# Attention units of batches 1 to 3: third tile first, 1/sum one unit later, two PSUM banks borrowed from the transposes

## The chip, the cores and the metric

The kernel runs on one core of a Trainium2 chip. The metric is the device time of one execution in microseconds (us), from launch to end on that core. TensorE is called PE below, its weight loads PEld, VectorE DVE, ScalarE ACT, GpSimd POOL, and SyncE (which only issues DMAs here) SP.

## The reference

The program computes an attention and two dense layers on top of it; shapes are q, k, v = (4 batches, 8 heads, 1152, 64).

```python
q_pool = q.reshape(B, H, S // 2, 2, D).mean(axis=3)        # 576 pooled queries
scores = scale * np.matmul(q_pool, k.transpose(0, 1, 3, 2))
attn = np.exp(scores - max) ; attn = attn / (attn.sum(-1) + 1e-9)
x = np.matmul(attn, v)                                     # heads side by side: (2304, 512)
h = x @ w_in ; g = where(h >= 1, h, where(h <= -1, 0, (h + 1) ** 2 / 4)) ; y = g @ w_out
out = np.maximum(np.maximum(y @ w1, y @ w2), y @ w3) @ w_out2
```

## The kernel before

**Units.** The attention is cut into 48 units: batch b (4), block i of 192 pooled queries (3), pair of heads p (4). A unit has three score tiles of 128 rows by 1152 keys. Tiles 0 and 1 hold 128 queries of one head each; tile 2 holds the remaining 64 queries of both heads. Numbers are kept as pairs of fp16 (a high part and a rest), so products are made of three matmuls.

**Words of a unit.** The order in which TensorE does the work is written out by hand as a string of words per unit (ORDER, line 31; the loop that reads it is at lines 621 to 656). Only TensorE is held to that order (ORDERED); the other engines' queues are laid out by the scheduler, by readiness and by the place in the program.

- `s0` and `s2` (qk, lines 369 to 384, and soft, 386 to 399): 12 score matmuls into one PSUM tile of three banks each (L378, then L383), per tile a row maximum on DVE (L395), a small scale on ACT (L396), and exp with its row sum on ACT (L397). `s0` makes tiles 0 and 1, `s2` makes tile 2. In `s0` the first three matmuls of L378 write tile 0, the next three tile 1.
- `t0`, `t1` (turned, lines 449 to 452), in batches 1 to 3: an fp16 copy of exp on ACT (L450), the rest on DVE (L451), and a transposing DMA on SP (L452) that puts both into `pt`, the transposed weights of the unit.
- `t2` (lines 427 to 441): nine transposes of exp on PE (L433) into a PSUM tile `tr`, then a copy to fp16 on ACT (L439) and the rest on DVE (L440). In batch 0 (WHOLE) all three tiles are turned in this way, with one f32 copy on ACT each (L444, L446).
- `r` (shares, lines 403 to 417): 1/sum of the unit. DVE adds and inverts (L408, L409), POOL spreads it over 64 columns (L411), PE transposes twice (L413, L414) into the unused end of the tile `tr`, columns 1152 to 1408, whose first part shares the third bank with the last transpose, and ACT copies it to `R` (L416, L417).
- `a1` (av, lines 456 to 491): the product of the unit before with v, 54 matmuls (L469), scaled by R into `xf` on DVE (L482). After the last pair of a block the block is split into fp16 `xh` on POOL (L274) and DVE (L275).
- `d`: one step of the first dense layer, 24 matmuls. An up step (L533) reads `xh` and is followed by ACT L537, DVE L538 and L539, ACT L540, DVE L541; a down step (L558) is half of an output tile, whose second half is followed by ACT L561 and L562 and a store. From unit 5 on, a unit's four `d` are up, up, down half, down half. The dense steps of block j begin with the first `d` of unit 4j+5.
- `q`: in odd units, load and preparation of the queries of the next two units. `w`: a step of the preparation of the dense weights.
- Loads and preparations of k and v of the next batch (k_steps, v_steps) are events at times 3n, 3n+1, 3n+2 of unit n, run by `now`.

**PSUM.** Score tiles and `tr` share a ring of two tiles of three banks (pss, tag sc); sums, `av` and the dense accumulators share two single banks (psg, tag g1). After the last unit one more `av` follows, then the dense steps that are left, with the weights of the second dense layer (L686, L161) beside them, and then that layer's matmuls (L777, L794).

The two orders, before:

```python
ORDER = {True: "s0 w0 d d w1 t0 a1 q t1 w2 s2 d d t2 w3 r",     # batch 0
         False: "s0 d t0 a1 t1 s2 q d d t2 r d"}                # batches 1 to 3
```

Of the kernel before, what the change touches and what calls it, by code (L numbers as in the profile page):

```python
# [7 lines left out]
F32 = mybir.dt.float32  # L8
# [3 lines left out]
AF = mybir.ActivationFunctionType  # L12
ALU = mybir.AluOpType
# [14 lines left out]

ORDER = {True: "s0 w0 d d w1 t0 a1 q t1 w2 s2 d d t2 w3 r",
         False: "s0 d t0 a1 t1 s2 q d d t2 r d"}
DEPTH = 1
DENSE = 5
LEAD = 12
# [1 line left out]
WHOLE = lambda b, p: b == 0  # L37
# [13 lines left out]
def body(ctx: ExitStack, tc: tile.TileContext, q, k, v, w_in, w_out, w1, w2, w3, w_o2, out):  # L51
    nc = tc.nc
    P = 128
# [9 lines left out]
    KT = S // P  # L63
    NCH = 3
# [9 lines left out]
    psg = ctx.enter_context(tc.tile_pool(name="psg", bufs=2, space=PSUM))  # L74
# [5 lines left out]
    @contextmanager  # L80
    def shift(n):
        n = max(n, -tc.cur_priority)
        tc.cur_priority += n
        yield
        tc.cur_priority -= n
# [59 lines left out]
    stk = at.enter_context(tc.tile_pool(name="stk", bufs=NPAIR, side="right"))  # L145
    ptp = at.enter_context(tc.tile_pool(name="ptp", bufs=2, side="right"))
    pss = at.enter_context(tc.tile_pool(name="pss", bufs=2, space=PSUM))
    def place(name):
        return pss.tile([P, NCH, 512], F32, tag="sc", name=name).rearrange("p a b -> p (a b)")

    def split_rows(hi, lo, st, s):

# [114 lines left out]
    units = [(b, i, p) for b in range(B) for i in range(NBL) for p in range(NPAIR)]  # L267
# [89 lines left out]
    def exp_scale(b, i, p):  # L357

        e = small.tile([P, 1], F32, tag="esc", bufs=3, name=f"esc{b}_{i}_{p}")
        nc.vector.scalar_tensor_tensor(out=e, in0=ub[b][:, p, 0:1], scalar=0.5 / float(D) ** 0.5, in1=esc[b, i, p],  # L360
                                       op0=ALU.mult, op1=ALU.mult)
        esc[b, i, p] = e

    PT, sums = {}, {}
# [4 lines left out]
    def qk(b, i, p, who):  # L369

        hh = qst[b, i, p]
        ks = kst[b, p].rearrange("p a b c -> p a (b c)")
        scs = [place(f"sc{b}_{i}_{p}_{w}")[:, :KT * P] for w in who]
        parts = [(sc, w, 0, P) for sc, w in zip(scs, who)] if len(who) > 1 else [(scs[0], h, 64 * h, 64) for h in range(2)]
        ww = 3 if len(who) > 1 else 4
        order = [(x, c) for x in parts for c in cuts] if len(who) > 1 else [(x, c) for c in cuts for x in parts]
        for (sc, h, m0, m), (n0, n1) in order:
            nc.tensor.matmul(sc[m0:m0 + m, n0:n1], hh[h if len(who) > 1 else who[0]][:, m0:m0 + m], ks[:, h, n0:n1],  # L378
                             start=True, stop=False)
        for n0, n1 in cuts:  # L380
            for sc, h, m0, m in parts:
                rows = slice(64 * h, 64 * h + 64)
                nc.tensor.matmul(sc[m0:m0 + m, n0:n1], hh[ww][rows, m0:m0 + m], ks[rows, h, n0:n1], start=False, stop=True)  # L383
        return scs

    def soft(b, i, p, who, sc):

        key = f"{b}_{i}_{p}_{who}"
        e = esc[b, i, p]
        st = small.tile([P, 2], F32, tag="st", bufs=3, name=f"st{key}")  # L390
        m, nb = st[:, 0:1], st[:, 1:2]
        if who == 0:
            sums[b, i, p] = small.tile([P, 3], F32, tag="sm", bufs=4, name=f"sm{b}_{i}_{p}")
        pf = pfp.tile([P, KT * P], F32, tag="pf", name=f"pf{key}")
        nc.vector.tensor_reduce(out=m, in_=sc, axis=AX.X, op=ALU.max, negate=True)  # L395
        nc.scalar.activation(out=nb, in_=m, func=AF.Copy, scale=e, bias=PS)  # L396
        nc.scalar.activation(out=pf, in_=sc, func=AF.Exp, bias=nb, scale=e,  # L397
                             accum_out=sums[b, i, p][:, who:who + 1])
        return b, i, p, who, pf

    R = {}

    def shares(b, i, p):

        sm = sums.pop((b, i, p))
        rs = R[b, i, p]
        R[b, i, p] = tp.tile([P, NB], F32, tag="R", bufs=3, name=f"R{b}_{i}_{p}")
        nc.vector.tensor_scalar(out=sm, in0=sm, scalar1=1e-9 * 2.0 ** 12, scalar2=None, op0=ALU.add)  # L408
        nc.vector.reciprocal(out=sm, in_=sm)  # L409
        rb = tp.tile([P, 2, 64], F32, tag="rb", bufs=2, name=f"rb{b}_{i}_{p}")  # L410
        nc.gpsimd.tensor_copy(out=rb, in_=sm[:, 0:2].rearrange("p (a o) -> p a o", o=1).to_broadcast([P, 2, 64]))  # L411
        r, half = R[b, i, p], slice(64, P)
        nc.tensor.transpose(rs[:, 0:P], rb.rearrange("p a o -> p (a o)"), ident)  # L413
        nc.tensor.transpose(rs[:, P:2 * P], sm[:, 2:3].to_broadcast([P, P]), ident)  # L414

        nc.scalar.activation(out=r, in_=rs[:, :NB], func=AF.Copy)  # L416
        nc.scalar.activation(out=r[half, P:NB], in_=rs[half, NB:2 * P], func=AF.Copy)  # L417

    def whole(pt):
        return pt.rearrange("p a b c -> p (a b c)").bitcast(F32).rearrange("p (h c n) -> p h c n", h=2, c=KT)  # L420

    def turned(b, i, p, who, pf):
        key = f"{b}_{i}_{p}_{who}"
        if who == 0:
            PT[b, i, p] = ptp.tile([P, 2, 2 * KT, NB], F16, tag="pt", name=f"pt_{b}_{i}_{p}")
        pt = PT[b, i, p]
        if who == 2 or WHOLE(b, p):

            tr = place(f"tr{key}")
            rs = tr[:, KT * P:KT * P + 2 * P]  # L430
            tr = tr[:, :KT * P]
            for c in range(KT):
                nc.tensor.transpose(tr[:, c * P:(c + 1) * P], pf[:, c * P:(c + 1) * P], ident)  # L433
            if who == 2:
                R[b, i, p] = rs
            if not WHOLE(b, p):
                tr = tr.rearrange("p (c h q) -> p h c q", c=KT, h=2)
                hi, lo = pt[:, :, 0:KT, P:NB], pt[:, :, KT:2 * KT, P:NB]
                nc.scalar.activation(out=hi, in_=tr, func=AF.Copy)  # L439
                nc.vector.tensor_tensor(out=lo, in0=tr, in1=hi, op=ALU.subtract)  # L440
                return
            pt = whole(pt)
            if who < 2:
                nc.scalar.activation(out=pt[:, who, :, 0:P], in_=tr.rearrange("p (c q) -> p c q", c=KT), func=AF.Copy)  # L444
            else:
                nc.scalar.activation(out=pt[:, :, :, P:NB], in_=tr.rearrange("p (c h q) -> p h c q", c=KT, h=2),  # L446
                                     func=AF.Copy)
            return
        hl = hlp.tile([P, 2, KT * P], F16, tag="hl", name=f"hl{key}")
        nc.scalar.activation(out=hl[:, 0], in_=pf, func=AF.Copy)  # L450
        nc.vector.tensor_tensor(out=hl[:, 1], in0=pf, in1=hl[:, 0], op=ALU.subtract)  # L451
        nc.sync.dma_start_transpose(out=pt[:, who, :, 0:P], in_=hl.rearrange("p a b -> p (a b)"))  # L452
# [154 lines left out]
    def now(t):  # L607
        for gen in events.get(t, ()):
            next(gen)
# [11 lines left out]
    def attend(n, word):  # L621

        b, i, p = units[n]
        kind, num = word[0], word[1:]
        if kind == "s":
            who = int(num)
            if who == 0:
                exp_scale(b, i, p)
            whos = (0, 1) if who == 0 else (2,)
            for w, sc in zip(whos, qk(b, i, p, whos)):  # L630
                behind[n, w] = soft(b, i, p, w, sc)
            now(3 * n + who)
        elif kind == "t":
            turned(*behind.pop((n, int(num))))
            if num == "1":
                now(3 * n + 1)
        elif kind == "r":
            shares(*units[n])
        elif kind == "a":
            if n >= int(num):  # L640
                av(*units[n - int(num)])
        elif kind == "d":
            if n >= DENSE:
                next(dense, None)
        elif kind == "q":
            if n % 2 == 1 and n + 1 < len(units):
                q_prep(*units[n + 1])
        elif kind == "w":
            if num in W_AT.get(n, ""):
                with shift(OW):  # L650
                    next(wgen, None)

    for n, (b, i, p) in enumerate(units):
        with tc.issue_after(issued["w" if n == 1 else "q"]) if n < LEAD else nullcontext():
            for word in ORDER[WHOLE(b, p)].split():
                attend(n, word)
    last = len(units)
    for n in range(last - DEPTH, last):
        av(*units[n])
    order.__exit__(None, None, None)  # L660
# [217 lines left out]
```

## Time and profile before

| | us |
|---|---|
| runs shown: median (lowest to highest of 3) | 1426.27 (1416.11 to 1430.86) |
| the profiled execution's own time | 1412.68 |
| its span, first to last instruction | 1410.9 |
| PE busy in the span | 1133.5 (80%) |
| DVE busy | 841.5 (60%) |
| ACT busy | 740.1 (52%) |
| POOL busy | 164.4 (12%) |
| mean granted TensorE clock, share of 2.4 GHz | 0.906 |

The span is divided as follows: units 0 to 11 (batch 0) until about 330 us, units 12 to 47 until 1047.6 us, the rest of the first dense layer and the weights of the second until 1121.6 us, and the second dense layer to the end. The engines run side by side, so a busy share is not a share of the time that could be saved.

### The profile page before, as it was taken

What the parts mean: (1) busy time and instruction counts of PE and PEld (TensorE: products, weight loads), DVE (VectorE), ACT (ScalarE), POOL (GpSimd) and SP (SyncE); (2) the same over time, 40 slices, a digit from 0 to 9 for tenths busy, and PEclk for the clock granted to TensorE, in tenths of its full rate; (3) what the DMA queues carried; (4) which work ended last, traced back from release to release, by engine and by line L of the source; (5) the groups of instructions that cost most, each with busy time, mean ns of one, the idle gap of its engine ahead of it and who ended that gap; (6) DMA issues with size and microseconds to landing.
All of it is one profiled execution on the core that took longest, in us unless ns stands there. A gap on an engine that the chain in (4) does not pass through costs nothing. (4 is left out here: it accounts for less than half of the span.)

```text
span 1410.9 us, 26612 instructions
## 1 busy us (share of the span) xinstructions
PE 1133.5 (80%) x11061; PEld 902.2 (64%) x11061; DVE 841.5 (60%) x1468; ACT 740.1 (52%) x1337; POOL 164.4 (12%) x200
## 2 busy tenths in 40 slices
PE   2467586987888786878887767888889799999998
PEld 1234364766766665666776656777779677677764
DVE  5964756558656667666665767665669865232221
ACT  5754766665555665556665646665656541111211
POOL 2210001122010112201011211000003102010000
PEclk9667787999989898889999989999989899999999
DMA  8832401246444447554445664344454421000001
GB/s 256 228 87 81 141 34 44 75 111 129 89 86 95 82 100 152 134 105 86 89 83 111 146 131 80 68 79 74 74 140 163 147 89 59 23 9 23 16 23 38
DMA packets 282201, 133.32 MB, mean 94 GB/s; under 512 B 240608, under 2 KB 265184, under 8 KB 281056
## 3 DMA queue, kind: packets, MB, share of 16 engines
q1 hardware_dynamic: 282080, 131.62, 39.8%
q8 instruction: 86, 1.41, 0.4%
q14 instruction: 35, 0.29, 0.1%
HBM read 62.39 MB, written 9.44 MB: 51 GB/s over the span
## 5 line engine op out<-in xcount | busy, mean ns | idle before, releaser
L395 DVE TENSOR_REDUCE st<-sc 128x1 f32<-128x1152 f32 x144 | 190.6, 1351 | 214.4 <-PE sc L383 214.4
L558 PE MATMUL py<-g,wou 128*128 128x192 f16 x2304 | 244.9, 274 | 6.6 <-ACT g L540 4.8
L558 PEld LDWEIGHTS <-wou 128*128 128x128 f16 x2304 | 227.5, 110 | 13.3 <-issue 7.3
L533 PE MATMUL ph<-xh,win 128*128 128x192 f16 x2304 | 210.3, 250 | 12.2 <-DVE xf L482 11.3
L777 PE MATMUL p<-yh,wm 128*128 128x288 f16 x1728 | 216.3, 287 | 3.6 <-POOL yh L748 3.6
L533 PEld LDWEIGHTS <-win 128*128 128x128 f16 x2304 | 193.2, 100 | 29.8 <-issue 29.1
L777 PEld LDWEIGHTS <-wm 128*128 128x128 f16 x1728 | 169.6, 98 | 49.9 <-issue 4.3
L397 ACT ACTIVATE pf<-sc,st,esc 128x1152 f32<-128x1152 f32 x144 | 188.4, 1309 | 3.5
L433 PE MATMUL tr<-ident,pf 128*128 128x128 f32 x648 | 100.2, 308 | 92.4 <-ACT pf L397 91.7
L433 PEld LDWEIGHTS tr<-ident,pf 128*128 128x128 f32 x648 | 81.8, 158 | 108.2 <-ACT pf L397 99.5
L413 PE MATMUL tr<-ident,rb 128*128 128x128 f32 x48 | 18.3, 380 | 132.4 <-DVE pt L440 90.4
L378 PE MATMUL sc<-kst,qst 128*64 128x512 f16 (+3 forms) x576 | 106.1, 366 | 11.6 <-DMA qst<-qpre 10.6
L396 ACT ACTIVATE st<-st,esc 128x1 f32<-128x1 f32 x144 | 41.7, 290 | 114.5 <-DVE st L395 114.2
L413 PEld LDWEIGHTS tr<-ident,rb 128*128 128x128 f32 x48 | 7.7, 161 | 143.9 <-issue 83.1
L451 DVE TENSOR_TENSOR hl<-pf,hl 128x1152 f16<-128x1152 f32 x72 | 97.7, 1357 | 1.0 <-ACT hl L450 1.0
L785 ACT ACTIVATE h<-mx 128x288 f16<-128x288 f32 x48 | 21.2, 442 | 132.7 <-DVE mx L783 132.7
L469 PE MATMUL av<-pt,vhl 128*64 128x192 f16 x1944 | 87.1, 247 | 4.1 <-DVE ub L93 4.1
L469 PEld LDWEIGHTS <-vhl 128*64 128x64 f16 x1944 | 80.3, 110 | 9.5 <-issue 9.5
L782 DVE TENSOR_TENSOR mx<-p,mx 128x288 f32<-128x288 f32 x48 | 21.8, 455 | 106.3 <-PE p L777 105.8
L450 ACT ACTIVATE hl<-pf 128x1152 f16<-128x1152 f32 x72 | 83.2, 1156 | 0.0
L378 PEld LDWEIGHTS <-qst 128*64 128x64 f16 (+1 forms) x576 | 47.5, 116 | 47.2 <-issue 21.7
L541 DVE SCALAR_TENSOR_TENSOR g<-t,dgs,g 128x384 f16<-128x384 f32 x96 | 62.2, 650 | 15.0 <-ACT g L540 15.0
(174 smaller groups left out, 1507.6 us busy)
## 6 DMA issues: line engine op xcount, KB each, us to landing
kn<-in_k_dram SPq DMA_DIRECT2D x16, 576.0 KB, 4.3
vn<-in_v_dram SPq DMA_DIRECT2D x16, 576.0 KB, 4.4
raw_m<-in_moe_w_dram SPq DMA_DIRECT2D x12, 768.0 KB, 4.4
raw_in<-in_moe_w_in_dram SPq DMA_DIRECT2D x8, 1024.0 KB, 5.6
qn<-in_q_dram SPq DMA_DIRECT2D x24, 256.0 KB, 3.3
raw_ou<-in_moe_w_out_dram SPq DMA_DIRECT2D x10, 512.0 KB, 4.5
y_d<-ys SPq DMA_DIRECT2D x48, 96.0 KB, 1.6
yf<-y_d SPq DMA_DIRECT2D x8, 576.0 KB, 3.7
```

The lines of the kernel that those rows point to most:

```text
L378: nc.tensor.matmul(sc[m0:m0 + m, n0:n1], hh[h if len(who) > 1 else who[0]][:, m0:m0 + m], ks[:, h, n0:n1], start=True, stop=False)
L395: nc.vector.tensor_reduce(out=m, in_=sc, axis=AX.X, op=ALU.max, negate=True)
L396: nc.scalar.activation(out=nb, in_=m, func=AF.Copy, scale=e, bias=PS)
L397: nc.scalar.activation(out=pf, in_=sc, func=AF.Exp, bias=nb, scale=e, accum_out=sums[b, i, p][:, who:who + 1])
L433: nc.tensor.transpose(tr[:, c * P:(c + 1) * P], pf[:, c * P:(c + 1) * P], ident)
L450: nc.scalar.activation(out=hl[:, 0], in_=pf, func=AF.Copy)
L451: nc.vector.tensor_tensor(out=hl[:, 1], in0=pf, in1=hl[:, 0], op=ALU.subtract)
L469: nc.tensor.matmul(acc[64 * h:64 * h + 64], vhl[b, p][:, vi, h, c, :], pt[:, h, pi * KT + c, :], start=(c == 0 and e == 0), stop=(c == KT ...
L533: nc.tensor.matmul(ph[:, a], win[:, wi, kt, ff * P:(ff + 1) * P], x[:, xi, kt], start=(kt == 0 and e == 0), stop=(kt == KD - 1 and e == 2))
L541: nc.vector.scalar_tensor_tensor(out=g[:, 1, fs, :], in0=t2, scalar=gs, in1=g[:, 0, fs, :], op0=ALU.mult, op1=ALU.subtract)
L558: nc.tensor.matmul(py, wou[:, ff // 2, wi, ff % 2, m * P:(m + 1) * P], g[:, gi, ff, :], start=(ff == 0 and e == 0), stop=(ff == NF - 1 and ...
L777: nc.tensor.matmul(ph[:, :NB2], wm[:, wi, i, kt, ff * P:(ff + 1) * P], yh[:, yi, kt, n0:n0 + NB2], start=(kt == 0 and e == 0), stop=(kt == ...
```

## The change

For batches 1 to 3 a unit now begins with tile 2: its scores, its transposes, then 1/sum of the unit before, and only then the two copies of the transposed tile (word `c2`); tiles 0 and 1 follow, with the product of the unit before. In batch 0 1/sum of the unit before comes after `s0`. The transposes of 1/sum go to the free end of the tile `tr` of the unit that is running, or, in batch 0, to one bank of psg. The events of k and v, which stood behind the `s` words and behind `t1`, are words of their own (`n0`, `n1`, `n2`). The last unit's 1/sum is made after the loop, in a tile of its own.

```diff
-ORDER = {True: "s0 w0 d d w1 t0 a1 q t1 w2 s2 d d t2 w3 r",
-         False: "s0 d t0 a1 t1 s2 q d d t2 r d"}
+ORDER = {True: "s0 n0 w0 r d d w1 t0 a1 q t1 n1 w2 s2 n2 d d t2 w3",
+         False: "s2 n0 q d d t2 r c2 n1 d s0 n2 t0 t1 a1 d"}
+ORDER_FIRST = {True: 0, False: 2}
...
-    def place(name):
-        return pss.tile(...)
+    spare = [None]
+
+    def place(name, keep=False):
+        x = pss.tile([P, NCH, 512], F32, tag="sc", name=name).rearrange("p a b -> p (a b)")
+        if keep:
+            spare[0] = x[:, KT * P:KT * P + 2 * P]
+        return x
...
-        rs = R[b, i, p]
+        rs = spare[0] if spare[0] is not None else psg.tile([P, 512], F32, tag="g1", name=f"rs{b}_{i}_{p}")
...
-            tr = place(f"tr{key}")
-            rs = tr[:, KT * P:KT * P + 2 * P]
-            tr = tr[:, :KT * P]
+            tr = place(f"tr{key}", not WHOLE(b, p))[:, :KT * P]
...
-                nc.scalar.activation(out=hi, in_=tr, func=AF.Copy)
-                nc.vector.tensor_tensor(out=lo, in0=tr, in1=hi, op=ALU.subtract)
+
+                def copies():
+                    nc.scalar.activation(out=hi, in_=tr, func=AF.Copy)
+                    nc.vector.tensor_tensor(out=lo, in0=tr, in1=hi, op=ALU.subtract)
+                late_copies.append(copies)
                 return
...
         elif kind == "r":
-            shares(*units[n])
+            if n:
+                shares(*units[n - 1])
+        elif kind == "c":
+            late_copies.pop()()
+        elif kind == "n":
+            now(3 * n + int(num))
...
     last = len(units)
+    place("rs_last", True)
+    shares(*units[last - 1])
     for n in range(last - DEPTH, last):
         av(*units[n])
```

## Rows read from the trace of the kernel before

**Rows 1.** The page, part 1: busy time and share of the span by engine.

```profile
PE 1133.5 (80%) x11061; PEld 902.2 (64%) x11061; DVE 841.5 (60%) x1468; ACT 740.1 (52%) x1337; POOL 164.4 (12%) x200
```

**Rows 2.** Windows of the units: length, busy time by engine, granted clock, DMA.

```profile
core 0: us, PE busy (x) PEld busy (x) DVE busy (x) ACT busy (x) POOL busy (x), PEclk, DMA share, GB/s
355.40:470.60 115.20, 96.97 (x1110) 80.65 (x1111) 72.34 (x115) 69.03 (x132) 10.14 (x16) 0.91 0.46 89
470.60:610.80 140.20, 106.87 (x1126) 89.89 (x1127) 93.47 (x164) 79.03 (x148) 24.37 (x29) 0.87 0.58 121
610.80:724.60 113.80, 95.56 (x1110) 79.89 (x1111) 72.33 (x115) 69.02 (x132) 10.14 (x16) 0.93 0.46 88
724.60:862.60 138.00, 102.42 (x1126) 86.40 (x1126) 93.69 (x164) 79.16 (x148) 24.60 (x29) 0.90 0.57 117
862.60:1047.60 185.00, 155.63 (x1850) 130.31 (x1851) 116.66 (x171) 113.73 (x214) 9.17 (x16) 0.95 0.42 81
...
938.50:956.10 17.60, 14.76 (x185) 12.42 (x185) 11.27 (x16) 11.30 (x21) 0.29 (x1) 1.00 0.44 80
```

**Rows 3.** Waits of PE in 332.9 to 1047.6 us: total, times, longest.

```profile
PE tr L413 <- DVE pt L440: 87.7, 30, 4.1
...
PE tr L413 <- POOL qpre L344: 10.9, 3, 4.0
```

**Rows 4.** Timeline of one unit without loads: start, length, engine, line, idle before it.

```profile
938.51 0.30 PE L413 MATMUL tr<-ident,rb 128*128 128x128 f32 x1 [2.71 <-DVE pt L440]
...
940.74 1.14 PE L378 MATMUL sc<-kst,qst 128*128 128x512 f16 x6
...
942.40 2.15 PE L533 MATMUL ph<-xh,win 128*128 128x192 f16 x24
...
948.80 6.08 SPq L452 DMA_TRANSPOSE pt<-hl  x2
...
952.23 1.20 PE L433 MATMUL tr<-ident,pf 128*128 128x128 f32 x9 [0.17 <-ACT pf L397]
...
953.47 1.13 ACT L439 ACTIVATE pt<-tr 128x1152 f16<-128x1152 f32 x1
...
954.64 1.36 DVE L440 TENSOR_TENSOR pt<-tr,pt 128x1152 f16<-128x1152 f32 x1 [0.50 <-ACT pt L439]
```

**Rows 5.** Groups by line, ACT: busy time, mean ns of one, idle before.

```profile
L416 ACT ACTIVATE R<-tr 128x192 f32<-128x192 f32 x48 | 15.9, 331 | 86.1 <-PE tr L414 86.1
...
L417 ACT ACTIVATE R<-tr 64x64 f32<-64x64 f32 x48 | 10.5, 219 | 1.5
...
L537 ACT ACTIVATE t<-ph,Uv 128x384 f32<-128x384 f32 x96 | 54.5, 570 | 5.2 <-PE ph L533 4.8 <-DVE g L541 0.4
...
L540 ACT ACTIVATE g<-t,dgs 128x384 f16<-128x384 f32 x96 | 58.4, 610 | 21.0 <-DVE t L539 20.9
...
L561 ACT ACTIVATE ys<-py,yd 128x192 f32<-128x192 f32 x48 | 20.1, 419 | 73.4 <-PE py L558 70.3 <-DMA y_d<-ys 2.9
L562 ACT ACTIVATE py<-py,yd 128x192 f32<-128x192 f32 x48 | 18.6, 387 | 0.0
```

**Rows 6.** Waits of PE in batch 0, 43.4 to 332.9 us.

```profile
PE tr L433 <- ACT pf L397: 58.4, 14, 9.3
PE tr L413 <- POOL rb L411: 10.9, 3, 5.2
PE tr L413 <- ACT pt L446: 9.2, 7, 1.3
```

**Rows 7.** Timeline of a unit that ends a block: xf to xh.

```profile
910.36 1.99 POOL L274 TENSOR_SCALAR xh<-xf,Uv 128x768 f16<-128x768 f32 x1 [11.74 <-DVE xf L482]
...
912.76 1.00 DVE L275 SCALAR_TENSOR_TENSOR xh<-xf,Uv,xh 128x768 f16<-128x768 f32 x1
```

**Rows 8.** Timeline behind the last unit: end of its scores, first preparation of w1.

```profile
1033.87 2.15 PE L533 MATMUL ph<-xh,win 128*128 128x192 f16 x24
...
1051.18 1.69 ACT L161 ACTIVATE st_m<-raw_m 128x768 f32<-128x768 f32 x2 [2.29 <-DMA pt<-hl]
```

More of the change, by code (lines that the diff above doesn't have):

```diff
@@ L147, in body @@
     pss = at.enter_context(tc.tile_pool(name="pss", bufs=2, space=PSUM))
-    def place(name):
-        return pss.tile([P, NCH, 512], F32, tag="sc", name=name).rearrange("p a b -> p (a b)")
+    spare = [None]
[4 more added lines that the diff above has]
+        return x
     def split_rows(hi, lo, st, s):
@@ L391, in soft @@
         m, nb = st[:, 0:1], st[:, 1:2]
-        if who == 0:
+        if (b, i, p) not in sums:
             sums[b, i, p] = small.tile([P, 3], F32, tag="sm", bufs=4, name=f"sm{b}_{i}_{p}")
@@ L420, in whole @@
         return pt.rearrange("p a b c -> p (a b c)").bitcast(F32).rearrange("p (h c n) -> p h c n", h=2, c=KT)
+    late_copies = []
     def turned(b, i, p, who, pf):
         key = f"{b}_{i}_{p}_{who}"
-        if who == 0:
+        if (b, i, p) not in PT:
             PT[b, i, p] = ptp.tile([P, 2, 2 * KT, NB], F16, tag="pt", name=f"pt_{b}_{i}_{p}")
@@ L427, in turned @@
         if who == 2 or WHOLE(b, p):
-            tr = place(f"tr{key}")
-            rs = tr[:, KT * P:KT * P + 2 * P]
-            tr = tr[:, :KT * P]
+            tr = place(f"tr{key}", not WHOLE(b, p))[:, :KT * P]
             for c in range(KT):
                 nc.tensor.transpose(tr[:, c * P:(c + 1) * P], pf[:, c * P:(c + 1) * P], ident)
-            if who == 2:
-                R[b, i, p] = rs
             if not WHOLE(b, p):
@@ L626, in attend @@
             who = int(num)
-            if who == 0:
+            if who == ORDER_FIRST[WHOLE(b, p)]:
                 exp_scale(b, i, p)
@@ L631, in attend @@
                 behind[n, w] = soft(b, i, p, w, sc)
-            now(3 * n + who)
         elif kind == "t":
             turned(*behind.pop((n, int(num))))
-            if num == "1":
-                now(3 * n + 1)
         elif kind == "r":
-            shares(*units[n])
+            if n:
[4 more added lines that the diff above has]
+            now(3 * n + int(num))
         elif kind == "a":
```

## The prediction

> **What bounds the kernel now.** I read the busy shares first, then windows of groups of units, then PE's waits, then the timeline of one unit. PE is the busiest engine with 80%, DVE has 60%, ACT 52% [rows 1]. A full PE is not what sets the time in the attention, though: there PE's waits and its clock do. The units fall into two groups. In 22 of them (14 to 19, 26 to 31, 38 to 47) no k or v is prepared: three windows of 115.2, 113.8 and 185.0 us, 414.0 in all, 18.82 us a unit, of which PE is busy 348.2 / 22 = 15.83 us. The other windows hold 12 units with k and v work, (140.2 + 138.0) / 12 = 23.18 us each, with PE busy 17.4, DVE 15.6 and ACT 13.2 us [rows 2]. One unit with nothing extra took 17.60 us with PE busy 14.76 us at a granted clock of 1.00 [rows 2]. So a plain unit loses 18.82 - 17.60 = 1.2 us on average, nearly all of it (15.83 - 14.76 = 1.07) because the same matmuls ran part of the time at the lower of PE's two clock levels, 1.2 instead of 2.4 GHz; the windows show 0.87 to 0.95 [rows 2].
>
> The largest wait of PE in units 12 to 47 is that of the 1/sum transpose L413, 87.7 us in 30 times on DVE L440 and 10.9 us on POOL [rows 3], about 2.7 us in nearly every unit. The timeline shows how it comes about: the nine transposes of tile 2 end at 952.23 + 1.20 = 953.43; ACT copies them (L439, 1.13), DVE takes the rest (L440, 1.36), ending at 956.00, and only then, at 956.1, do the two small transposes into the same tile begin (the window of the plain unit runs from one L413 to the next [rows 2]). One unit earlier the same wait stands at 938.51 with 2.71 us. Before L433 PE waited only 0.17 us [rows 4]: from the end of s0 to there PE and the chain of ACT are equally long, 952.23 - 942.40 = 9.83 us.
>
> **The change: which work moves.** Read as a ring, the unit before is s0, d, a1, s2, d, d, t2, r, d; after it is s0, a1, d, s2, d, d, t2, r, d. PE's instructions are the same in number and size. What changes is that r no longer waits for the copies, that the copies wait for r, and that ups and downs change places.
>
> *Waits that go and come.* The wait of 2.71 us goes. Next late is the fourth matmul of s0, which writes the slot of `tr` and has to wait for L440 and for the copies of R. From the end of t2 on: r's transposes 0.41 (0.30 plus the second's start, taken at 0.11), a semaphore step 0.15, R's copies 0.331 + 0.219 = 0.55 [rows 5], L439 1.13, a step of 0.04, L440 1.36, a step of 0.14: 3.78 us (the steps as in the timeline, 953.47 + 1.13 to 954.64 and 956.00 to 956.1). Beside it PE has r and one down step, 940.74 - 938.51 = 2.23 us, and the first half of L378, 1.14 / 2 = 0.57: 2.80 us [rows 4]. The new wait is at least 3.78 - 2.80 = 0.98 us.
>
> The two up steps now both stand just ahead of t2, so that their ACT work ends up beside the copies: L540 costs 0.61 and L537 0.57 [rows 5]. With none between, the gain is 2.71 - 0.98 = 1.73; with one L540, 1.12; with L537 and L540, 0.55. I take the middle one, 1.12 us, as the two jobs of the earlier up step should be done by then.
>
> *The bank.* That L413 waited for L440, although they touch different columns, shows that accesses to one bank are kept apart [rows 3, 4]. The Trainium skill (PSUM — Partial Sum Buffer, section PSUM bank collisions raise a hardware error) says that two engines must not touch the same bank and quadrant at once, reads included, whatever the address. By that rule the change does not get rid of the dependency but turns it round: r and the copies of R, 0.41 + 0.55 us, now stand ahead of L439. By the rule the sum below holds; if the copies could run beside r, some 0.96 us a unit, 34 us over 35 units, would come on top. The trace agrees with the rule for one direction only (L413 behind L440).
>
> *ACT's chain from s0 to t2.* Two up halves' work (L537, L540, L537: 1.75) gives place to L561, L562 and one L537 (0.42 + 0.39 + 0.57 = 1.38, and the read of a sum) [rows 5]. That is no longer than now, so t2 still waits about 0.17.
>
> *Clock.* The longest wait of a plain unit goes from 2.7 to about 1.6 us, and the stretch of small transposes and wait around it is broken up by a down step. If that ends the time at 1.2 GHz, a plain unit gains 1.07 us more; if not, 0. I take three quarters, 0.8: the plain unit of 17.60 us kept its 2.4 GHz even with the longer wait [rows 2], so the shorter one should seldom lose it.
>
> *Sum for the plain units.* 22 x (1.12 + 0.8) = 42.2 us; bounds 22 x 0.55 = 12 and 22 x (1.73 + 1.07) = 62.
>
> *Units with k and v, and unit 13.* 13 units, where DVE and ACT are fuller and set more of the time. The second step of v (an ACT pass, nearest row L439 with 1.13 us) now comes ahead of the product that frees its buffer, nine times, and has to wait for it. I take half of the plain gain, 0.96 x 13 = 12.5 us; bounds -6.5 (half a us lost in each) and 1.92 x 13 = 25.
>
> *Batch 0.* r moves behind the next unit's s0. There PE waits above all for exp (58.4 us), and for 1/sum 10.9 us on POOL and 9.2 on L446 [rows 6]. The 20.1 us of the last two go, but the fourth matmul of s0 then waits for L446 (nearest row: L439, 1.13 us). I take 10 us; bounds 0 and 20. The bank that r takes from psg there is free again after R's copies (0.55), while two d of 2.15 follow: nothing.
>
> *xh.* The first up step of a block stood one d, s0 and more behind the product that completes xh. Now a down step and s2 lie between: 2.15 + some 1.3 = 3.45 us. The way from xf to xh is POOL 1.99, then DVE until 912.76 + 1.00 = 913.76, 3.4 us after POOL's start at 910.36 [rows 7], plus xf itself and steps, some 0.6: 4.0. PE waits 0.6 us, up to one L440-sized DVE job more (1.36). I take 1.0 us for each of nine blocks: -9; bounds 0 and -18.
>
> *The end.* Tiles 0 and 1 of the last unit are now the last to be made. From the end of their scores (1033.87) to when the last transposing DMA had landed and ACT could use the buffers for the weights of the next layer (1051.18) went 17.3 us [rows 8]. After the change PE has only one product and one d (some 4.6 us) to put there; four dense steps that are left (8.6) may fill part. I take -7; bounds 0 and 17.3 - 4.6 = -13.
>
> *DMA and POOL queues.* The two transposes of a unit (6.08 us for both [rows 4]) are now issued at its end and read by the product one unit later, some 16 us: hidden, and if that cover went, the product would wait. The loads of q, k and v and the stores keep their places in the ring to within one d; on POOL the spread of 1/sum comes a unit late and is no longer awaited. All cost nothing.
>
> *Total.* 42.2 + 12.5 + 10 - 9 - 7 = 48.7 us off the profiled execution's 1412.7 (its span and 1.8 us around it): 1364. The extremes add up to 1412.7 - 107 = 1306 and 1412.7 + 25.5 = 1438. The median of the runs lies 13.6 us above that execution. If it is time at the lower clock, most of it goes with the waits; I leave a quarter, 3.4, and predict 1367.
>
> **The rivals.** *B, more than that:* nothing stands between r and the copies and the clock stays at full: 62 + 25 + 15 - 9 - 7 = 86, 1327 us. For it: in the unit of 17.60 us all the rest is PE work. Against: the ACT work of two up steps.
>
> *C, the wait only moves:* two ACT jobs stand ahead of L439 and the clock gains nothing: 12 + 0 + 10 - 9 - 7 = 6, and with the 13.6 us of the runs 1420. For it: ACT is busy 11.3 of 17.6 us even in the emptiest unit [rows 2].
>
> *D, slower:* the first up step of a unit needs one of two banks of psg. One holds the product, free once xf is taken; the other the output of the down step that ended only s2 earlier and is free after L561 and L562. If the step gets that one, it waits for ACT. The exp of tile 2 ends 952.23 - 0.17 - 942.40 = 9.66 us after s0; behind L561 and L562 still come L537 (0.57) and that exp (nearest row L439, 1.13), so they would end some 8.0 us after s0, where PE arrives two steps ahead of t2, at 9.83 - 2 x 2.15 = 5.5 [rows 4, 5]. A wait of 2.5 us against the 1.12 won loses 1.4 x 35 = 48 us; 10 are won in batch 0, 7 lost at the end, no clock is won: 45 over 1412.7, with the runs' 13.6, 1471 us. It decides once that wait exceeds 1.12 us. Against it: xf frees the other bank some 2 us earlier; which bank a step gets, no row shows.
>
> **How the numbers follow.** My forecast 0.62, B 0.16, C 0.13, D 0.09. About 1% is what a measurement of this kernel can tell. C lies within 1%, as does the upper edge of mine (0.02), some of C is better than its price (0.02), and D is slower: faster 0.78, same 0.13, slower 0.09. The range is 1320 to 1410: B lies inside at its lower end, D and most of C are left out, as are the extremes, which all terms would have to reach together.
>
> **What would show it.** Right: no wait of L413 on DVE L440; in plain units a wait of L378 of 1.0 to 1.6 us on L440 or L417 instead; clock of the plain windows above 0.95; a plain unit of 16 to 17 us. Waits of L533 on xh, nine, up to 2 us. Wrong: L533 waiting on L562 in every unit (D), L433 waiting longer on exp (C), or a clock as before with 17.6 us units.

## The result and the profile after

The changed kernel took 1340.4 us in the median of 4 runs (1338.96 to 1343.65), against 1425.15 in the median of 4 for the kernel before: 0.941 of its time, 95% interval 0.936 to 0.947, or 85 us less. The prediction was 1367 us in a range of 1320 to 1410.

The profiled execution of the changed kernel took 1343.65 us with a span of 1341.9, which is 69.0 us less than the span before. That is less than the 85 us of the medians, because the profiled execution before (1412.7) lay 12.5 us below its kernel's median and that of the changed kernel lies 3.3 above. Where the 69.0 us come from, measured between the starts of the nine transposes of tile 2 of the units named:

| stretch | before | after | difference |
|---|---|---|---|
| start to unit 0 | 39.3 | 39.8 | +0.5 |
| unit 0 to 11 (batch 0) | 269.6 | 260.9 | -8.7 |
| unit 11 to 12 (these transposes now stand first in the unit) | 18.9 | 8.5 | -10.4 |
| unit 12 to 47 | 715.9 | 641.9 | -74.0 |
| unit 47 to the end | 367.2 | 390.8 | +23.6 |

The waits of PE in units 12 to 47 of the changed kernel (lines of the changed file: L384 and L389 are the score matmuls, L419 the 1/sum transposes, L439 the transposes of tile 2, L445 and L446 its copies):

```profile
PE sc L384 <- DVE pt L446: 40.4, 31, 1.8
PE tr L439 <- ACT pf L403: 24.7, 18, 4.4
PE av L476 <- DVE ub L94: 19.7, 8, 2.5
PE ph L540 <- DVE xh L281: 3.3, 3, 1.1
```

The 1/sum transposes, 98.6 us in the two lines of [rows 3], wait for nothing any more in these units. In their place the second half of the scores of s0 waits for the copies, 40.4 us in 31 times. The wait of the product (L476) for DVE L94, which was 4.1 us in 9 times before, has grown to 19.7 us in 8 times, in the units with k and v. The windows of 21 plain units, which answer to [rows 2] (cut at the transposes of tile 2 in place of L413), after:

```profile
core 0: us, PE busy (x) PEld busy (x) DVE busy (x) ACT busy (x) POOL busy (x), PEclk, DMA share, GB/s
332.60:429.90 97.30, 88.31 (x1112) 74.73 (x1110) 73.59 (x115) 69.71 (x133) 9.40 (x14) 1.00 0.57 111
561.70:661.10 99.40, 89.97 (x1113) 76.40 (x1111) 74.33 (x115) 70.18 (x134) 9.39 (x14) 0.98 0.56 107
789.30:934.80 145.50, 132.33 (x1667) 112.26 (x1666) 109.07 (x162) 103.40 (x193) 10.43 (x16) 1.00 0.52 90
```

They add up to 342.2 us, 16.30 a unit. The same 21 units, cut in the same way, before:

```profile
core 0: us, PE busy (x) PEld busy (x) DVE busy (x) ACT busy (x) POOL busy (x), PEclk, DMA share, GB/s
351.40:466.70 115.30, 97.02 (x1110) 80.72 (x1110) 72.21 (x116) 69.05 (x132) 10.14 (x16) 0.91 0.46 88
606.90:720.70 113.80, 95.56 (x1111) 79.89 (x1111) 72.17 (x116) 69.04 (x132) 10.14 (x16) 0.93 0.45 88
858.70:1024.40 165.70, 139.22 (x1665) 116.83 (x1665) 105.39 (x158) 102.45 (x193) 8.88 (x15) 0.96 0.42 77
```

That is 394.8 us, 18.80 a unit. PE is busy 14.79 us a unit (310.6 / 21) where it was 15.80 (331.8 / 21), for the same matmuls: the granted clock, 0.91 to 0.96 before, is at 0.98 to 1.00. So a plain unit gained 2.50 us, of which 1.0 is the clock and 1.5 is waiting.

A plain unit of the changed kernel, from the transposes of tile 2 on, which answers to [rows 4]:

```profile
869.75 1.15 PE L439 MATMUL tr<-ident,pf 128*128 128x128 f32 x9
...
870.74 0.27 PE L419 MATMUL tr<-ident,rb 128*128 128x128 f32 x1
...
871.37 0.31 ACT L422 ACTIVATE R<-tr 128x192 f32<-128x192 f32 x1
...
871.72 0.22 ACT L423 ACTIVATE R<-tr 64x64 f32<-64x64 f32 x1
871.96 0.61 ACT L547 ACTIVATE g<-t,dgs 128x384 f16<-128x384 f32 x1
872.60 1.13 ACT L445 ACTIVATE pt<-tr 128x1152 f16<-128x1152 f32 x1
...
872.93 0.65 PE L384 MATMUL sc<-kst,qst 128*128 128x512 f16 x3
873.76 1.36 DVE L446 TENSOR_TENSOR pt<-tr,pt 128x1152 f16<-128x1152 f32 x1 [0.54 <-ACT pt L445]
875.17 0.65 PE L384 MATMUL sc<-kst,qst 128*128 128x512 f16 x3 [1.59 <-DVE pt L446]
```

The 1/sum transposes follow the nine at once. Then come R's two copies on ACT, one L547 of the dense layer, and only then the copies of tile 2: from the end of the nine (870.90) to the fourth score matmul (875.17) 4.27 us pass, and PE stands still for the last 1.59 of them. This is the chain of the prediction with one L540 in it (3.78 + 0.61 = 4.39).

### The profile page after: what moved, and what is told of

Read it like the earlier page. It is cut to its first block, busy times and chain, and to the rows that moved or that the text cites. A ratio compares the mean times of both kernels' runs of the same rounds, so it can differ in the third digit from the quotient of the medians.

```text
span 1341.9 us, 26586 instructions
## 1 busy us (share of the span) xinstructions
PE 1111.8 (83%) x11061; PEld 891.7 (66%) x11061; DVE 846.5 (63%) x1468; ACT 743.7 (55%) x1337; POOL 166.2 (12%) x200
## 5 line engine op out<-in xcount | busy, mean ns | idle before, releaser
L540 PE MATMUL ph<-xh,win 128*128 128x192 f16 x2304 | 209.6, 252 | 20.0 <-ACT R L423 8.5
L565 PE MATMUL py<-g,wou 128*128 128x192 f16 x2304 | 217.1, 255 | 3.4 <-DVE g L548 2.7
L540 PEld LDWEIGHTS <-win 128*128 128x128 f16 x2304 | 197.9, 101 | 30.2 <-issue 27.7
L565 PEld LDWEIGHTS <-wou 128*128 128x128 f16 x2304 | 201.2, 102 | 11.8 <-issue 4.8
L439 PE MATMUL tr<-ident,pf 128*128 128x128 f32 x648 | 102.5, 313 | 84.8 <-ACT pf L403 84.8
L384 PE MATMUL sc<-kst,qst 128*128 128x512 f16 (+3 forms) x576 | 102.0, 345 | 62.5 <-DVE pt L446 41.9
L439 PEld LDWEIGHTS tr<-ident,pf 128*128 128x128 f32 x648 | 84.6, 161 | 97.0 <-ACT pf L403 88.0
L476 PE MATMUL av<-pt,vhl 128*64 128x192 f16 x1944 | 96.4, 261 | 19.9 <-DVE ub L94 19.7
L384 PEld LDWEIGHTS <-qst 128*128 128x128 f16 (+1 forms) x576 | 41.9, 107 | 102.4 <-issue 71.9
L476 PEld LDWEIGHTS <-vhl 128*64 128x64 f16 x1944 | 89.2, 118 | 27.0 <-issue 26.9
L417 POOL COPY rb<-sm 128x128 f32<-128x128 f32 x48 | 22.8, 475 | 392.8 <-DVE sm L415 372.5
L389 PE MATMUL sc<-kst,qst 64*128 64x512 f16 (+3 forms) x576 | 66.6, 338 | 0.0
```

The costliest lines, as they stand in the source:

```text
L476: nc.tensor.matmul(acc[64 * h:64 * h + 64], vhl[b, p][:, vi, h, c, :], pt[:, h, pi * KT + c, :], start=(c == 0 and e == 0), stop=(c == KT ...
L540: nc.tensor.matmul(ph[:, a], win[:, wi, kt, ff * P:(ff + 1) * P], x[:, xi, kt], start=(kt == 0 and e == 0), stop=(kt == KD - 1 and e == 2))
L565: nc.tensor.matmul(py, wou[:, ff // 2, wi, ff % 2, m * P:(m + 1) * P], g[:, gi, ff, :], start=(ff == 0 and e == 0), stop=(ff == NF - 1 and ...
```

## The experiments

Two theories stood against each other at first. W: the gain is the wait of r behind the copies and the clock that it costs. O: the gain is the order, with tile 2 first and both up steps ahead of its transposes. Four kernels were to tell them apart and to price the shared bank and batch 0.

**Copies first again (e1_copies_first).** In the changed kernel:

```diff
-         False: "s2 n0 q d d t2 r c2 n1 d s0 n2 t0 t1 a1 d"}
+         False: "s2 n0 q d d t2 c2 r n1 d s0 n2 t0 t1 a1 d"}
```

> The changed kernel with r and c2 exchanged in batches 1 to 3, so that the two transposes of 1/sum stand behind the copies of tile 2 again; all else of the change stays. Theory W (the gain is the wait of r behind the copies, 2.7 us a unit, and the clock that it costs): the wait of L419 on DVE L446 comes back with about 2.7 us in each of 36 units, and because ACT also has the work of two up steps there, up to 3.3; the wait of L384 goes; plain units 17.5 to 18.3 us at a granted clock of 0.9 to 0.97; about 1405 to 1425 us. Theory O (the gain is the order, tile 2 first with both up steps ahead of its transposes): the time stays near 1340 to 1360 us.

One run took 1431.8 us (before, beside it, 1424.2), 7 us above the range expected: the whole gain was gone. Its waits of PE, over the whole span, and a window of five plain units:

```profile
PE tr L419 <- DVE pt L446: 108.7, 36, 4.8
PE tr L439 <- ACT pf L403: 86.3, 35, 7.6
PE av L476 <- DVE ub L94: 19.7, 8, 2.5
```

```profile
core 0: us, PE busy (x) PEld busy (x) DVE busy (x) ACT busy (x) POOL busy (x), PEclk, DMA share, GB/s
353.20:448.50 95.30, 78.88 (x929) 65.99 (x926) 61.29 (x98) 57.81 (x113) 8.08 (x12) 0.95 0.45 85
```

The wait of the 1/sum transposes is back in all 36 units, 3.0 us each. A plain unit took 18.99 us, about as before the change (18.80), and the clock was down again, 0.93 to 0.95 in windows of such units. All the rest of the change was still in this kernel, so the order alone wins nothing: units 12 to 47 took 735.2 us, 19 more than before. O falls.

**The old order, copies behind r (e2_old_order).** In the kernel before:

```diff
-         False: "s0 d t0 a1 t1 s2 q d d t2 r d"}
+         False: "s0 d t0 a1 t1 s2 q d d t2 r c2 d"}
...
-                nc.scalar.activation(out=hi, in_=tr, func=AF.Copy)
-                nc.vector.tensor_tensor(out=lo, in0=tr, in1=hi, op=ALU.subtract)
+
+                def copies():
+                    nc.scalar.activation(out=hi, in_=tr, func=AF.Copy)
+                    nc.vector.tensor_tensor(out=lo, in0=tr, in1=hi, op=ALU.subtract)
+                late_copies.append(copies)
...
```

> The kernel before with one edit: the copies of tile 2 come behind r (1/sum of the same unit, not of the unit before), in batches 1 to 3; tile 2 stays last and batch 0 stays as it was. Theory W: r waits at most some 0.3 us for 1/sum, which was ready about when the nine transposes ended (L409 952.83, POOL's spread until 953.44, transposes until 953.43), the copies start some 1 us later, and the fourth matmul of s0 waits 1.0 to 1.8 us; plain units 16.2 to 16.8 us at full clock; no loss of some 13 us at the end of the attention and no gain of 9 us in batch 0: about 1335 to 1350 us. Theory O: most of the gain is gone, 1390 us or more.

1332.2 us (1331.9 to 1333.2), 0.936 of before (0.932 to 0.940): a little below the range expected, and 8 us less than the changed kernel. Plain units took 16.31 us, as in the changed kernel (16.30). Tile 2 need not come first, and 1/sum need not be that of the unit before, although 1/sum of the same unit is waited for a little more than expected: L413 waits for POOL 12.6 us in 12 times in units 12 to 47. In the profiles the changed kernel is 9 us shorter than this one in batch 0 (260.9 against 269.7) and 18 us longer behind it (1041.2 against 1022.8 from unit 11 to the end).

**A bank of its own (e3_own_bank).** In the changed kernel:

```diff
-        rs = spare[0] if spare[0] is not None else psg.tile([P, 512], F32, tag="g1", name=f"rs{b}_{i}_{p}")
+        rs = psg.tile([P, 512], F32, tag="g1", name=f"rs{b}_{i}_{p}")
...
-    place("rs_last", True)
```

> The changed kernel with the transposes of 1/sum in a bank of psg in batches 1 to 3 too, so that the copies of tile 2 share no bank with them. If the copies start late because the bank is shared (theory W with the bank rule): the wait of L384 in a plain unit falls from 1.3 to 1.6 us to about 0.4 to 0.7, as 0.41 of transposes and 0.55 of R's copies drop out ahead of L445 as far as ACT has no other work; 25 to 35 us less than the changed kernel, unless the two banks of psg, which now serve a fifth tile a unit, make an up or down step wait. If ACT's other work sets the start of the copies (rival): the wait stays at 1.3 or more and the time within 5 us of the changed kernel's 1340, or some us slower by waits for a psg bank.

1294.4 us (1293.4 to 1294.9), 0.909 of before (0.906 to 0.913): 46 us less than the changed kernel, more than expected. Plain units 15.36 us. The waits of PE in units 12 to 47:

```profile
PE av L476 <- DVE ub L94: 19.7, 8, 2.5
PE tr L439 <- ACT pf L403: 19.4, 15, 3.5
PE sc L384 <- DVE pt L446: 7.8, 17, 0.6
```

The wait for the copies went from 40.4 to 7.8 us, at most 0.6 each. A plain unit shows how:

```profile
829.68 1.15 PE L439 MATMUL tr<-ident,pf 128*128 128x128 f32 x9
...
831.30 1.11 ACT L445 ACTIVATE pt<-tr 128x1152 f16<-128x1152 f32 x1
...
832.31 0.32 ACT L422 ACTIVATE R<-rs 128x192 f32<-128x192 f32 x1
832.45 1.36 DVE L446 TENSOR_TENSOR pt<-tr,pt 128x1152 f16<-128x1152 f32 x1 [0.31 <-ACT pt L445]
832.52 0.61 ACT L547 ACTIVATE g<-t,dgs 128x384 f16<-128x384 f32 x1
...
833.86 0.65 PE L384 MATMUL sc<-kst,qst 128*128 128x512 f16 x3 [0.34 <-DVE pt L446]
```

The copies now come ahead of R's first copy and of the L547 that stood before them. From the end of the nine (830.83) to the fourth score matmul (833.86) 3.03 us pass instead of 4.27. So it was not ACT's other work that held the copies back, but what they shared with 1/sum: the tile `tr`, and in it the third bank. Which of the two counts, this run does not tell, since it takes 1/sum out of both.

**Batch 0 as before (e4_batch0_old).** In the changed kernel, 1/sum of batch 0 at the end of its own unit and in the end of tr:

```diff
-ORDER = {True: "s0 n0 w0 r d d w1 t0 a1 q t1 n1 w2 s2 n2 d d t2 w3",
+ORDER = {True: "s0 n0 w0 d d w1 t0 a1 q t1 n1 w2 s2 n2 d d t2 w3 r",
...
-            tr = place(f"tr{key}", not WHOLE(b, p))[:, :KT * P]
+            tr = place(f"tr{key}", who == 2)[:, :KT * P]
...
-            if n:
-                shares(*units[n - 1])
+            u = units[n if WHOLE(b, p) else n - 1]
+            if u in sums:
+                shares(*u)
```

> The changed kernel with 1/sum of batch 0 as before: at the end of its own unit and in the end of the tile tr. The change's part in batch 0, measured between the third transposes of units 0 and 11, was 8.7 us shorter than before. If that part gives this: 1347 to 1351 us, and the waits of 1/sum on L453 and POOL are back in batch 0. Rival (batch 0 is set by the weights' preparation, and the 8.7 us are scatter): the same time as the changed kernel within 4 us.

1345.4 us (1341.5 to 1349.7), 0.945 of before (0.941 to 0.950). In the profile the stretch from unit 0 to 11 is back at 269.0 us (before 269.6, changed 260.9), so the change's part in batch 0 gives about 8 us there. The waits of 1/sum on L453 (12.0 us in 7 times) and on POOL (5.6 in 2) are back as well. The times of the two kernels, whose runs overlap, say 5 us, between the two expectations, and do not settle it.

With W standing and the shared tile end dearer than thought, the next questions were whether the new order is worth anything once the bank is out of the way, what the new wait in the k and v units costs, and where the loss at the end comes from.

**Old order, own bank, 1/sum a unit late (e5_old_order_own_bank).** In the changed kernel, with the edit of e3_own_bank and:

```diff
-         False: "s2 n0 q d d t2 r c2 n1 d s0 n2 t0 t1 a1 d"}
-ORDER_FIRST = {True: 0, False: 2}
+         False: "s0 n0 r d t0 a1 t1 n1 s2 n2 q d d t2 c2 d"}
+ORDER_FIRST = {True: 0, False: 0}
```

> Own bank for 1/sum and tile 2 last again: batches 1 to 3 go s0, r of the unit before (into a bank of psg), d, t0, a1, t1, s2, q, d, d, t2, copies, d; batch 0 as in the changed kernel. Theory W (wait and bank are the whole gain; tile 2 first costs some 8 us, as the second run showed against the changed kernel, most of it behind the last unit): e3_own_bank's 1294 less 5 to 13, 1281 to 1289 us; plain units 15.0 to 15.8. Theory O (tile 2 first helps once the bank is out of the way, because 1/sum is off the chain and the transposes of tiles 0 and 1 have a unit's time): slower than 1294 by 5 us or more.

1286.0 us (1282.6 to 1288.8), 0.904 (0.900 to 0.909): as W expected, 8 us less than with tile 2 first. Here an up step waits for R's copies out of the bank of psg (whole span; 18.2 us in 9 times of it in units 12 to 47):

```profile
PE ph L540 <- ACT R L423: 29.4, 14, 3.5
```

What this place of r costs in time was not measured by itself.

**The event behind the product (e6_events_late).** In the changed kernel:

```diff
-         False: "s2 n0 q d d t2 r c2 n1 d s0 n2 t0 t1 a1 d"}
+         False: "s2 n0 q d d t2 r c2 n1 d s0 t0 t1 a1 n2 d"}
```

> The changed kernel with the event n2 (sum of k's squares, norm of v) behind a1 instead of ahead of it. In the changed kernel a1 waits 2.46 us for DVE L94, which frees the bank of that sum, in 8 units (19.7 us). If PE sets the time of those units: the wait goes and 12 to 20 us with it, 1320 to 1328. If ACT and DVE set it there: the wait of L439 on exp grows by what a1 gains, 1336 to 1344.

1327.9 us (1326.8 to 1330.0), 0.934 (0.929 to 0.939): 12.5 us less, as the first expectation said. The wait of the product for L94, 19.7 us, is gone. Not all of it was won: the score matmuls now wait longer for the copies, over the whole span 41.9 us in the changed kernel and here

```profile
PE sc L384 <- DVE pt L446: 69.6, 36, 4.5
```

**Another order for the last unit (e7_last_unit).** In the changed kernel:

```diff
+LAST = "s0 n0 d t0 t1 n1 s2 n2 q d d t2 r a1 c2 d"
...
-            if who == ORDER_FIRST[WHOLE(b, p)]:
+            if who == (0 if n == len(units) - 1 else ORDER_FIRST[WHOLE(b, p)]):
...
-            for word in ORDER[WHOLE(b, p)].split():
+            for word in (LAST if n == len(units) - 1 else ORDER[WHOLE(b, p)]).split():
```

> The changed kernel with the last unit alone in another order: tiles 0 and 1 first, tile 2 behind them, 1/sum of the unit before ahead of a1. Measured from the transposes of tile 2 of the last unit the changed kernel loses 23.6 us against before, of which 10.4 is where these transposes stand in the unit; the rest, 13 us, I put down to tiles 0 and 1 of the last unit being made last. If so: 8 to 13 us less than the changed kernel, 1327 to 1333. If the loss comes from DVE's work on the next layer's weights, which begins when the attention's buffers come free: 0 to 5 us less.

1334.6 us (1332.6 to 1335.1), 0.938 (0.934 to 0.943): 6 us less, between the two expectations. About half of the 13 us is the order of the last unit. The rest need not be the new order's: the kernels that keep tile 2 last, e2, e5 and e8, also take 371.9, 371.9 and 374.1 us from the transposes of unit 47 to the end, 5 to 7 more than the 367.2 before. Why they do stays open.

**The bank alone (e8_only_bank).** In the kernel before, one line (it moves 1/sum of batch 0 as well, which the expectation leaves out):

```diff
-        rs = R[b, i, p]
+        rs = psg.tile([P, 512], F32, tag="g1", name=f"rs{b}_{i}_{p}")
```

> The kernel before with one line changed: 1/sum is transposed into a bank of psg instead of the end of tr; order, batch 0 and all else as before. Theory W with the bank rule: L413 no longer waits for L440 (only up to 0.8 us for POOL), the copies start at the end of the transposes, the fourth matmul of s0 waits under 1 us; plain units 15.2 to 16.2 at full clock; 1290 to 1315 us. If 1/sum of the same unit is too late for that place (POOL's spread behind exp, the reason to take it from the unit before): waits of L413 on L411 of 1 us and more in most units, 1320 us or more.

1278.8 us (1277.2 to 1281.9), 0.900 of before (0.894 to 0.905): the fastest of all, below the range expected, and 62 us less than the changed kernel. Plain units took 15.42 us on average, and 15.01 in most of those where no q is prepared. One of these:

```profile
827.58 1.20 PE L433 MATMUL tr<-ident,pf 128*128 128x128 f32 x9 [0.17 <-ACT pf L397]
...
828.22 0.62 ACT L540 ACTIVATE g<-t,dgs 128x384 f16<-128x384 f32 x1 [0.69 <-DVE t L539]
828.50 0.29 POOL L411 COPY rb<-sm 128x128 f32<-128x128 f32 x1 [14.72 <-DVE sm L409]
828.82 1.13 ACT L439 ACTIVATE pt<-tr 128x1152 f16<-128x1152 f32 x1
...
828.85 0.33 PE L413 MATMUL rs<-ident,rb 128*128 128x128 f32 x1
...
829.98 1.36 DVE L440 TENSOR_TENSOR pt<-tr,pt 128x1152 f16<-128x1152 f32 x1 [0.49 <-ACT pt L439]
...
831.10 1.14 PE L378 MATMUL sc<-kst,qst 128*128 128x512 f16 x6
```

The copy on ACT and the 1/sum transpose on PE now start together at 828.8. L440 ends at 831.34, which is before PE has done the first three of the six score matmuls; nothing waits. 1/sum of the same unit, spread by POOL at 828.50, is there just in time; in other units it is not, in units 12 to 47:

```profile
PE rs L413 <- POOL rb L411: 9.8, 11, 1.8
```

The window of 9 plain units shows what is left:

```profile
core 0: us, PE busy (x) PEld busy (x) DVE busy (x) ACT busy (x) POOL busy (x), PEclk, DMA share, GB/s
751.90:888.30 136.40, 133.02 (x1665) 111.96 (x1666) 105.37 (x158) 101.47 (x193) 8.88 (x15) 1.00 0.51 93
```

PE is busy 133.0 of 136.4 us, at full clock. In the stretches of the table above, this kernel took 250.1 us in batch 0 (269.6 before), 595.2 in units 12 to 47 (715.9), and 374.1 from unit 47 to the end (367.2). So the one line also won 19.5 us in batch 0, more than the edits that the change makes there.

**Bank and event (e9_bank_and_event).** e8_only_bank, with the events of k and v as words at their old places and in batches 1 to 3 the last of them one dense step later:

```diff
...
-         False: "s0 d t0 a1 t1 s2 q d d t2 r d"}
...
+         False: "s0 n0 d t0 a1 t1 n1 s2 q d n2 d t2 r d"}
...
```

> The kernel before with 1/sum in a bank of psg and, in batches 1 to 3, the event n2 (sum of k's squares, norm of v) one dense step later, so that this step no longer waits for the bank of the product (L533 on DVE L482, 15.4 us in 7 units of e8_only_bank). If PE sets the time of those units: 5 to 15 us less than e8_only_bank's 1278.8. If DVE does, which is late with L482 there: within 4 us of it.

1287.1 us (1285.3 to 1288.6), 0.904 (0.898 to 0.910): 8 us more than e8_only_bank, which neither expectation allowed for. The wait moved to the following down step, and grew (waits of PE over the whole span, where e8_only_bank has 15.4 us of L533 on DVE L482):

```profile
PE py L558 <- ACT t L537: 26.6, 7, 4.3
```

Only 4.0 of the 7.7 us between the two profiles lie in units 12 to 47; 2.7 lie in batch 0, where the order did not change. So this wait explains the loss in part.

**All parts on the new order (e10_all_on_new_order).** The changed kernel with the edits of e3_own_bank, e6_events_late and e7_last_unit together.

> The changed kernel with the three parts that helped it one by one: own bank (46 us), n2 behind a1 (12 us), the last unit in another order (6 us). If they add up: 1340.4 - 64 = 1276 us, level with e8_only_bank, and tile 2 first is worth nothing by itself. If tile 2 first helps once its own faults are gone: 1270 or less. If the event's 12 us were won only beside the waits for the copies, as ACT and DVE are fuller now: 1282 to 1290.

1286.7 us (1282.3 to 1293.6), 0.904 (0.896 to 0.912): the time of the third expectation. The parts do not add up, and tile 2 first does not beat the one line. Between the profiles the later event gives 2.9 us in units 12 to 46, where it gave 10.2 in e6, and the other last unit gives 3.5 us from there to the end, where it gave 8.0 in e7. That ACT and DVE are fuller, the reason given, was not tried. What stays open: whether accesses to one tile in different banks would be kept apart as well, since in all runs the 1/sum shares tile and bank or neither.

## Why the prediction was right, and where its sizes were off

The direction, the main wait and the clock were right; 1367 (1367.4 in the sum) was some 27 us too high. Of these, 20.3 lie in the sum (48.7 us taken, 69.0 measured between the two profiled executions), and 6.7 in the step from one execution to the median, where 3.4 us were left on and 3.3 should have come off. The terms did not all err one way: the plain units gave 13 us more than taken and the units with k and v 15 more, batch 0 gave 1 less and the end lost 6 more.

- **The wait that goes.** Right. L413's 98.6 us [rows 3] went, and e1_copies_first brought them back with the time.
- **The wait that comes.** Right in place and nearly in size: 40.4 us in 31 times, at most 1.8; in the 21 plain units 1.4 each, where 1.6 was taken. L413 had waited 2.8 us in each of these, not 2.71, so the gain from both was 1.5 us a plain unit, 1.12 had been taken.
- **Clock.** Right, and almost complete: 1.0 of the 1.07 us came back, three quarters had been taken. With the waits a plain unit gave 2.50 us instead of 1.92, some 55 instead of 42 for the 22.
- **The bank.** The prediction took from the rule of the Trainium skill (PSUM — Partial Sum Buffer, section PSUM bank collisions raise a hardware error) that the dependency turns round, and put copies that could run beside r at 34 us over 35 units. The traces agree as far as they go. Before, L413 waits for L440. After, L445 stands behind R's copies in ACT's queue; no row shows L445 itself waiting for them, but once 1/sum has gone elsewhere (e3_own_bank) it comes first. That was worth 46 us. The 34 counted the 0.96 us of the chain and not the dense work of ACT (L547) that slips in while the copies wait. What is not shown is that the bank is what the two share: all columns of 1/sum, 1152 to 1408, lie in the third bank of `tr`, and they also lie in the same tile. Where a tile is handed on to the next use, the traces show that the whole of it counts: in the kernel before, the fourth matmul of s0, which writes columns 0 to 511, once in units 12 to 47 waits for L417, which reads only the third bank:

```profile
PE sc L378 <- ACT R L417: 0.4, 1, 0.4
```

- **Units with k and v, unit 13 and xh.** This is the term that was off most: 74.0 - 55 = 19 us measured, 12.5 - 9 = 3.5 taken. The twelve units with that work took 278.3 us before and 260.0 after, 1.5 us less each, where 0.96 was taken; unit 13 gained 0.3. (Ten of the twelve gained 0.7 each, 23.62 to 22.91, and the two at the edge, 19 and 31, went from 21.04 to 15.43. But the cut falls at the transposes of tile 2, which stand last in the unit before and first after, so it moves a unit's k and v work into the next stretch, and this split is not a comparison of the same work.) The waits for xh were 3.3 us, not 9. What still held these units back was not the buffer of v, which was named and for which ACT waited 4.1 us in 4 times in all, but the bank of psg: n2 puts the sum of k's squares just ahead of the product, which waits 2.46 us for DVE to read it. e6_events_late prices it at 12.5 us.
- **Batch 0.** 8.7 us in the profile, 10 taken.
- **The end.** 13 us lost (23.6 less the 10.4 of the shifted transposes), 7 taken, with 13 as the bound. e7_last_unit accounts for 6; 5 to 7 are also lost by the kernels that keep the old order.
- **The rivals.** C and D did not come: the plain units' clock rose, and in units 12 to 47 an up step waited for L569 once, 0.3 us. B, 1327, was 13 us too low. It was right on the clock; that nothing would stand between r and the copies was wrong, as L547 does.

## What to carry to other kernels

When a small result is put into the free end of a PSUM tile that others still read, look at what shares that tile and its bank: here the saved bank cost PE a wait of 2.8 us in a plain unit, and one line that took another tile in another bank gave 145 us (1423.6 to 1278.8), more than the rewritten order that the wait had called for. Ask of a wait what it is that the two operations share before moving the work around it. And when a reordering wins, put its edits into the old order one by one: here the exchange of r and the copies alone took 1332 us, and the rest of the reordering, with what it won in batch 0, cost 8.

## What the runs showed that had not been expected

- A wait of PE of 2.8 us in each plain unit went with a granted clock of 0.91 to 0.96; 1.4 us each, at most 1.8, went with 0.98 to 1.00, in the old order too (e2_old_order, 0.99 to 1.00); and where the long wait came back (e1_copies_first) the clock was 0.93 to 0.95. So a wait shorter by 1.5 us also gave back 1.0 us of PE's time in a plain unit, the same matmuls at 2.4 instead of 1.2 GHz. A single wait need not do it: the unit of [rows 4] kept 1.00 with 2.71 us. Why the clock falls after one such wait and not after another is not shown.
- The scatter between executions was smaller with shorter waits: 14.8 us between the lowest and highest of 4 before, 4.7 after. Longer runs of the kernel before had the lower clock (1413.8 us at 0.905, 1432.6 at 0.888), as they would if the scatter were mostly time at the lower clock. But e10_all_on_new_order scattered by 11.3 us with shorter waits, and this was not tried by itself.
